# Eighteen small unused loads beside the K and V stream of a decode step

## The chip, the cores and the metric

The kernel runs on one core of a Trainium2 chip. The metric is the device time of one execution in microseconds: median of three runs 195.51 us (195.49 to 195.56). Beside these runs there is one profiled execution, whose span from the first to the last instruction is 194.3 us.

## The reference

A decode step of a parallel block: a layer norm of x (4 batch rows of 512), then attention and a gated feed-forward from the same normalised row, both added to x.

```
W = min(4096, max(256, Sk // 4))            # Sk = 16384, so the last 4096 positions
q = (xn @ wq) in 32 heads of 128            # wq 512 x 4096
k, v = the last W of k_cache, v_cache       # 4 x 8 heads x 4096 x 128, each serves 4 query heads
o = softmax(q k^T / sqrt(128)) v
out = x + o @ wo + (silu(xn @ w_gate) * (xn @ w_up)) @ w_down    # 512 x 1792, 1792 x 512
```

Everything is bfloat16. One execution reads each cached row once: 81 MB, most of them K and V.

## The kernel before

The 32 pairs of batch row and K/V head are taken two at a time, so there are ND = 16 steps. A step loads one K tile and one V tile of 2,048 KB each (128 partitions, 32 positions of 128 numbers for each of two batch rows). K has two buffers (`kbuf`), V two (`vbuf`). In a step TensorE transposes K through an identity (line 397) into PSUM, VectorE copies it to `kT` (line 311), TensorE multiplies with the queries into `ps_s`, takes a row maximum, ScalarE makes the exponential (line 282), and TensorE multiplies with V into `ps_o`. The steps overlap: the product with V of one step runs between the transposes and the scores of the next.

Who issues what, and in which order, is written out by hand. SyncE issues nearly all loads on its own queue: the query weights `wq_sb` (128 partitions of 16,384 numbers, line 253), K 0 and K 1, gate and up weights, V 0, then in a loop `load_k(d)`, `load_v(d - 1)` for d = 2 to 15, the down weights, V 15, and the output weights in five cuts (line 251). `load_k` waits until TensorE has transposed the tile that lay in the buffer (`s_tr`), `load_v` until the product with the old V tile is done (`s_pv`). Both issue at line 177, in a helper. ScalarE issues the load of x and at the end the store of the output, four rows of 1,024 bytes. SyncE waits for that store last (line 512).

GpSimd sets up constants and masks and clears the first V buffer (lines 201 to 233) and has no work after that. `wq_sb` is read by the projection at the start; later its first 1,792 columns are reused for the gate and up products.

Of the kernel before, what the change touches and what calls it, by code (L numbers as in the profile page):

```python
# [12 lines left out]
def bass_parallel_sum__sliding_block_cached__swiglu_ffn__decode_kernel(  # L13
# [10 lines left out]
    out: bass.AP,  # L24
):
    B, _, D = A_x.shape
    _, HKV, Sk, Dh = A_k_cache.shape
    HQ = A_wq.shape[1] // Dh
    F = B_w_gate.shape[1]
# [26 lines left out]
    WQ = sb("wq_sb", [128, NC * HQ * Dh], BF16)  # L56
# [37 lines left out]
    I4 = sb("i4", [B, B], FP32)  # L94
    I4w = sb("i4w", [B, 64], BF16)
    y = sb("y_sb", [B, D], BF16)

    ps = nc.alloc_psum_tensor
    ps_kt = [ps("ps_kt%d" % s, [128, 512], FP32) for s in range(NG)]
# [15 lines left out]
    def sem(name):  # L115
        return nc.alloc_semaphore(name=name)
# [3 lines left out]
    d_wu = sem("d_wu")  # L120
    d_wd = sem("d_wd")
    d_out = sem("d_out")
    WO_CUTS = (0, 16, 22, 29, 31, 32)
    d_wo = [sem("d_wo%d" % q) for q in range(len(WO_CUTS) - 1)]
    d_k = [sem("d_k%d" % s) for s in range(2)]
# [21 lines left out]
    s_pv = sem("s_pv")  # L147
# [14 lines left out]
    wq_ap = A_wq.rearrange("(p c) n -> p (c n)", c=NC)  # L162
# [10 lines left out]
    def load(eng, to, rows, pieces):  # L173


        with nc.discard():
            by_row = eng.dma_start(to, rows).ins  # L177
        whole = replace(by_row.ins[0], ap=pieces.ap, bass_ap=pieces)
        return eng.add_instruction(replace(by_row, name=nc.get_next_instruction_name(), ins=[whole],
                                           ant_dge_precooked=False))  # L180

    def fold_rows(w):
        return w.rearrange("(p c) n -> p (c n)", p=32)

    def load_kv(eng, buf, cache, d):
        return load(eng, buf[:, d % 2 * KVN:(d % 2 + 1) * KVN], kv_ap(cache, d, 1), kv_ap(cache, d, FOLD))

    def out_rows(eng, c0, c1):
        for c in range(c0, c1):
            if c in WO_CUTS:  # L190
                eng.wait_ge(d_wo[WO_CUTS.index(c)], 16)
            for n in range(2):
                last = eng.matmul(ps_acc[64 * n:64 * n + B, 0:256], OP[:, c, :], WO[:, c, 256 * n:256 * n + 256],  # L193
                                  start=False, stop=True, skip_group_check=True)
        return last

    with nc.Block() as block:

        @block.gpsimd
        def _(eng):  # L200
            eng.memset(ident[:], 0.0)
            eng.memset(I4[:], 0.0)
            eng.memset(I8[:], 0.0)
            eng.memset(I4w[:], 0.0)
            eng.memset(rep[:], 0.0)
            eng.memset(ones[:], 1.0)
            eng.memset(mkr[:], -BIG)
            eng.memset(mkc[:], 1.0)
            eng.drain()
            eng.affine_select(I4[:], I4[:], pattern=[[-1, B]], compare_op=ALU.not_equal,  # L210
                              fill=1.0, base=0, channel_multiplier=1)
            eng.affine_select(ident[:], ident[:], pattern=[[-1, 128]], compare_op=ALU.not_equal,
                              fill=1.0, base=0, channel_multiplier=1)
            eng.affine_select(I8[:], I8[:], pattern=[[-1, C]], compare_op=ALU.not_equal,
                              fill=1.0, base=0, channel_multiplier=1)
            eng.affine_select(I4w[:], I4w[:], pattern=[[-1, 64]], compare_op=ALU.not_equal,
                              fill=1.0, base=0, channel_multiplier=1)

            eng.affine_select(rep[:], rep[:], pattern=[[1, REP], [-1, 128]], compare_op=ALU.not_equal,
                              fill=1.0, base=0, channel_multiplier=REP)  # L220

            eng.affine_select(mkr[:], mkr[:].rearrange("j (q b i) -> j q b i", b=2, i=FOLD),
                              pattern=[[0, 64 // FOLD], [-1, 2], [0, FOLD]], compare_op=ALU.not_equal,
                              fill=0.0, base=0, channel_multiplier=1)
            eng.affine_select(mkc[:], mkc[:].rearrange("j (b h) -> j b h", b=2),
                              pattern=[[-1, 2], [0, REP]], compare_op=ALU.is_equal,
                              fill=0.0, base=0, channel_multiplier=1)
            eng.memset(XnT[:].bitcast(FP32), 0.0)
            eng.memset(QZ[:].bitcast(FP32), 0.0)
            eng.drain()  # L230
            eng.engine_nop().then_inc(s_const, 1)
            eng.memset(P[:], 1.0)
            eng.memset(VB[:, HKN:].bitcast(FP32), 0.0)  # L233
            eng.drain()
            eng.engine_nop().then_inc(s_const, 1)
            eng.engine_nop().then_inc(d_v[1], 16)

        @block.sync
        def _(eng):
            def load_k(d):  # L240
                if d >= 2:
                    eng.wait_ge(s_tr, 2 * NG * (d - 1))
                load_kv(eng, KB, A_k_cache, d).then_inc(d_k[d % 2], 16)

            def load_v(d):
                eng.wait_ge(s_pv, d + 1)
                load_kv(eng, VB, A_v_cache, d).then_inc(d_v[d % 2], 16)

            def load_wo(n):
                a, b = WO_CUTS[n], WO_CUTS[n + 1]  # L250
                eng.dma_start(WO[:, a:b, :], wo_ap[:, a:b, :]).then_inc(d_wo[n], 16)  # L251

            eng.dma_start(WQ[:], wq_ap).then_inc(d_wq, 16)

            eng.wait_ge(s_xc, 1)
            load_k(0)
            load_k(1)
            load(eng, WG[:], wg_ap, fold_rows(B_w_gate)).then_inc(d_wg, 16)
            load(eng, WU[:], wu_ap, fold_rows(B_w_up)).then_inc(d_wu, 16)
            load_v(0)  # L260
            for d in range(2, ND):
                load_k(d)
                load_v(d - 1)
            load(eng, WD[:], wd_ap, fold_rows(B_w_down)).then_inc(d_wd, 16)
            load_v(ND - 1)
            for n in range(len(d_wo)):
                load_wo(n)
# [99 lines left out]
        def _(eng):  # L367
# [127 lines left out]
            eng.wait_ge(s_op, 1)  # L495
            out_rows(eng, 0, WO_CUTS[2])

# [6 lines left out]

    out_rows(nc.tensor, WO_CUTS[2], NO).then_inc(s_acc, 1)
    nc.vector.wait_ge(s_acc, 1)
# [2 lines left out]
    nc.scalar.activation(y[:, 256:512], ps_acc[64:64 + B, 0:256], ACT.Identity).then_inc(s_y, 1)  # L509
    nc.scalar.wait_ge(s_y, 2)  # L510
    nc.scalar.dma_start(out_ap, y[:]).then_inc(d_out, 16)
    nc.sync.wait_ge(d_out, 16)


# [26 lines left out]
```

## Time and profile before

| What | Value |
|---|---|
| time, median of 3 runs | 195.51 us |
| span of the profiled execution | 194.3 us |
| around the span, to that median | 1.2 us |
| TensorE matmuls busy | 84% of the span |
| VectorE busy | 59% |
| SyncE's queue q1, share of 16 DMA engines | 97.3% |
| read from memory | 81.01 MB, 417 GB/s over the span |
| mean granted TensorE clock | 0.991 |

The page gives the span of the profiled execution, and no time of its own beside it. Busy shares of a matmul engine include work that is pipelined. The sixteen DMA engines each have a ring for SyncE's queue; their share is the time that packets took, over sixteen times the span. A completion of a load is itself a small packet in these counts. The chain of waits follows the work that ended last back to the start, and a wait on a DMA in it covers the time from its issue to its landing, earlier loads in the same rings included.

### The profile page before, as it was taken

What the parts mean: (1) busy time and instruction counts of PE and PEld (TensorE: products, weight loads), DVE (VectorE), ACT (ScalarE), POOL (GpSimd) and SP (SyncE); (2) the same over time, 40 slices, a digit from 0 to 9 for tenths busy, and PEclk for the clock granted to TensorE, in tenths of its full rate; (3) what the DMA queues carried; (4) which work ended last, traced back from release to release, by engine and by line L of the source; (5) the groups of instructions that cost most, each with busy time, mean ns of one, the idle gap of its engine ahead of it and who ended that gap; (6) DMA issues with size and microseconds to landing.
All of it is one profiled execution on the core that took longest, in us unless ns stands there. A gap on an engine that the chain in (4) does not pass through costs nothing.

```text
span 194.3 us, 7749 instructions
## 1 busy us (share of the span) xinstructions
PE 164.1 (84%) x3460; PEld 142.1 (73%) x3461; DVE 115.4 (59%) x250; ACT 17.0 (9%) x27; POOL 10.5 (5%) x23
## 2 busy tenths in 40 slices
PE   0127999949999989898989898989898989898894
PEld 0112988848989878888878887888887888887662
DVE  1004757617677767676767676767676767675530
ACT  5700010100110101010101010101010101010100
POOL 8930000000000000000000000000000000000000
PEclk9999999988999999999999999999999999999999
DMA  6999997999999999999999999999999999999992
GB/s 217 432 432 432 511 452 332 432 437 432 425 432 425 432 432 432 438 445 432 432 432 432 438 432 438 432 438 432 432 432 432 445 432 432 432 428 428 401 400 94
DMA packets 3589, 81.09 MB, mean 417 GB/s; under 512 B 664, under 2 KB 800, under 8 KB 1184
## 3 DMA queue, kind: packets, MB, share of 16 engines
q1 hardware_dynamic: 3568, 81.01, 97.3%
q8 instruction: 4, 0.07, 0.1%
q10 hardware_dynamic: 16, 0.01, 0.0%
q14 instruction: 1, 0.01, 0.0%
HBM read 81.01 MB, written 0.00 MB: 417 GB/s over the span
## 4 chain that ended last, share of the span: by engine, by line
DMA 61%; PE 34%; issue 1%; DVE 1%; SPq 1%; DVEq 0%
DMA kbuf<-in_A_k_cache_dram 46%; PE ps_kt L397 18%; DMA wo_sb<-in_A_wo_dram 9%; PE ps_s L369 8%; DMA wq_sb<-in_A_wq_dram 6%; PE ps_o L369 5%; PE ps_kt L369 2%; PE ps_acc L369 1%; PE ps_acc L193 1%; DVE kT L311 1%; SPq L251 1%; DVE kT L299 0%; SPq L177 0%; DVE y_sb L507 0%; DVE qz L302 0%
## 5 line engine op out<-in xcount | busy, mean ns | idle before, releaser
L311 DVE COPY kT<-ps_kt 128x1024 bf16<-128x1024 bf16 x128 | 79.9, 683 | 27.4 <-PE ps_kt L397 27.3
L397 PE MATMUL ps_kt<-ident,kbuf 128*128 128x128 bf16 x1024 | 65.7, 225 | 10.4 <-DMA kbuf<-in_A_k_cache_dram 10.4
L397 PEld LDWEIGHTS ps_kt<-ident,kbuf 128*128 128x128 bf16 x1024 | 60.1, 101 | 15.8 <-issue 15.8
L369 PE MATMUL ps_o<-p,vbuf 128*128 128x64 bf16 x1120 | 39.2, 195 | 0.0
L369 PEld LDWEIGHTS ps_o<-p,vbuf 128*128 128x128 bf16 x1120 | 36.0, 99 | 1.2
L369 PEld LDWEIGHTS ps_s<-qz,kT 128*128 128x128 bf16 x1024 | 31.4, 98 | 6.7 <-issue 3.7
L369 PE MATMUL ps_s<-qz,kT 128*128 x1024 | 34.7, 192 | 1.2
L282 ACT ACTIVATE p<-ps_s 128x512 bf16<-128x512 f32 x17 | 10.2, 597 | 161.9 <-PE ps_s L369 161.9
L316 DVE TENSOR_REDUCE rm<-ps_s 128x8 bf16<-128x512 f32 x17 | 11.8, 691 | 19.8 <-PE ps_s L369 19.8
L369 PE MATMUL ps_o<-p,ones 128*128 128x128 bf16 (+1 forms) x69 | 7.0, 222 | 2.3 <-DVE qz L302 1.3
L369 PE MATMUL ps_kt<-wq_sb,xnT 128*32 128x512 bf16 x32 | 3.6, 629 | 5.3 <-DMA wq_sb<-in_A_wq_dram 5.3
L369 PEld LDWEIGHTS ps_o<-p,ones 128*128 128x128 bf16 x69 | 4.5, 98 | 3.5 <-issue 2.2
L369 PE MATMUL ps_s<-mkc,mkr 2*128 2x512 bf16 x17 | 6.9, 404 | 0.0
L374 PE MATMUL ps_acc<-i,xn 4*128 4x4 f32 x4 | 0.6, 254 | 7.4 <-ACT xn L279 7.4
L369 PE MATMUL ps_s<-dg,ones 8*128 8x512 bf16 x17 | 6.5, 385 | 0.0
L327 DVE TENSOR_REDUCE den<-ps_o 128x8 f32<-128x128 f32 x18 | 5.0, 275 | 2.5 <-PE ps_o L369 2.5
L369 PEld LDWEIGHTS ps_kt<-wq_sb,xnT 128*32 128x32 bf16 x32 | 1.2, 138 | 6.8 <-issue 6.8
L299 DVE STREAM_TRANSPOSE kT<-ps_kt 128x512 f32<-128x512 f32 x2 | 1.4, 717 | 8.0 <-PE ps_kt L369 8.0
L374 PEld LDWEIGHTS ps_acc<-i,xn 4*128 4x128 f32 x4 | 0.6, 207 | 7.3 <-issue 7.3
L233 POOL MEMSET vbuf<- 128x6144 f32 x1 | 5.2, 5222 | 0.0
L321 DVE TENSOR_REDUCE m<-ps_acc 8x1 f32<-8x128 f32 x17 | 4.6, 270 | 0.3 <-PE ps_acc L369 0.3
L331 DVE TENSOR_TENSOR oT<-ps_o,den 128x8 f32 (+1 forms) x18 | 3.0, 166 | 2.9 <-issue 2.7
(68 smaller groups left out, 48.6 us busy)
## 6 DMA issues: line engine op xcount, KB each, us to landing
kbuf<-in_A_k_cache_dram SPq DMA_DIRECT2D x16, 2048.0 KB, 12.5
vbuf<-in_A_v_cache_dram SPq DMA_DIRECT2D x16, 2048.0 KB, 11.2
wq_sb<-in_A_wq_dram SPq DMA_DIRECT2D x1, 4096.0 KB, 12.3
wo_sb<-in_A_wo_dram SPq DMA_DIRECT2D x1, 2048.0 KB, 14.9
wg_sb<-in_B_w_gate_dram SPq DMA_DIRECT2D x1, 1792.0 KB, 24.2
wu_sb<-in_B_w_up_dram SPq DMA_DIRECT2D x1, 1792.0 KB, 27.6
wd_sb<-in_B_w_down_dram SPq DMA_DIRECT2D x1, 1792.0 KB, 14.9
wo_sb<-in_A_wo_dram SPq DMA_DIRECT2D x1, 896.0 KB, 17.8
```

Source lines behind the costliest of these rows:

```text
L193: last = eng.matmul(ps_acc[64 * n:64 * n + B, 0:256], OP[:, c, :], WO[:, c, 256 * n:256 * n + 256], start=False, stop=True, skip_group_che ...
L233: eng.memset(VB[:, HKN:].bitcast(FP32), 0.0)
L251: eng.dma_start(WO[:, a:b, :], wo_ap[:, a:b, :]).then_inc(d_wo[n], 16)
L282: eng.activation(P[:, d % 2 * PS:d % 2 * PS + SN], ps_S[d % 2][:], ACT.Exp, scale=SCALE).then_inc(s_p, 1)
L299: eng.transpose(qT[:, 512 * n:512 * n + 512], ps_kt[n][:])
L311: eng.tensor_copy(KT[:, u * HKN + 1024 * g:u * HKN + 1024 * (g + 1)], kt_ps[g].rearrange("p a b -> p (a b)")).then_inc(s_ev, 1)
L316: eng.tensor_reduce(RM[:], ps_S[bank][:].rearrange("p (t c) -> p c t", c=C), AX.X, ALU.max).then_inc(s_rm, 1)
L321: eng.tensor_reduce(m8[:], mt_ps, AX.X, ALU.max)
L327: eng.tensor_reduce(den[:], den_ps.rearrange("p (t c) -> p c t", c=C), AX.X, ALU.add)
L331: eng.tensor_tensor(OT[:, 2 * b:2 * b + 2, ds(r * REP, REP)], O_ps.rearrange("p (j h) -> p j h", j=2), den[:].rearrange("p (j h) -> p j h" ...
L369: return eng.matmul(o, l, r, start=start, stop=stop, skip_group_check=True)
L397: last = eng.transpose(kt_ps[g][:, k, :], KB[:, a:a + 128], ident[:])
```

## The change

SyncE gets fourteen more loads, one after each `load_v(d - 1)` of its loop. They read the first columns of the first n rows of the query weights in memory, and write partitions 0 to n - 1 of a stretch of `wq_sb` that nobody reads any more: n is 1 to 13, and 15 in the last round, and a row has 64 + 16n numbers (160 to 608 bytes). All count on one semaphore, for which SyncE waits at the end of the program, ahead of its wait for the output. GpSimd gets four: 3, 5, 7 and 2 partitions with two pieces each of 96, 104, 112 and 120 bytes, each behind a wait for the products with V of steps 5 to 8; they have a semaphore for which nobody waits. No load of the change is used by the computation, and nothing is removed.

```
@@ names
+    scr = WQ[0:16, 4096:8192]
+    scw = WQ[0:16, 8192:9216]
...
@@ gpsimd, at its end
             eng.engine_nop().then_inc(d_v[1], 16)
+            at = 0
+            for i, n in enumerate((3, 5, 7, 2)):
+                eng.wait_ge(s_pv, 6 + i)
+                w = 48 + 4 * i
+                eng.dma_start(scw[0:n, at:at + 2 * w].rearrange("p (a b) -> p a b", b=w),
+                              wq_ap[0:n, 0:512].rearrange("p (a b) -> p a b", b=256)[:, :, 0:w]).then_inc(d_scw, 16)
+                at += 2 * w
@@ sync
             load_v(0)
+            at = 0
             for d in range(2, ND):
                 load_k(d)
                 load_v(d - 1)
+                n = d - 1 if d < 15 else 15
+                w = 64 + 16 * n
+                eng.dma_start(scr[0:n, at:at + w], wq_ap[0:n, 0:w]).then_inc(d_scr, 16)
+                at += w
             load(eng, WD[:], wd_ap, fold_rows(B_w_down)).then_inc(d_wd, 16)
...
     nc.scalar.dma_start(out_ap, y[:]).then_inc(d_out, 16)
+    nc.sync.wait_ge(d_scr, 16 * 14)
     nc.sync.wait_ge(d_out, 16)
```

On SyncE, the end of its loop (`wd_sb` are the down weights, `wo_sb` the output weights), before:

```order
L177 DMA kbuf<-in_A_k_cache_dram 128x1x8192
L177 DMA vbuf<-in_A_v_cache_dram 128x1x8192
L177 DMA wd_sb<-in_B_w_down_dram 128x7168
L177 DMA vbuf<-in_A_v_cache_dram 128x1x8192
L251 DMA wo_sb<-in_A_wo_dram 128x8192
```

and with the change:

```order
L278 DMA wq_sb<-in_A_wq_dram 13x272
L181 DMA kbuf<-in_A_k_cache_dram 128x1x8192
L181 DMA vbuf<-in_A_v_cache_dram 128x1x8192
L278 DMA wq_sb<-in_A_wq_dram 15x304
L181 DMA wd_sb<-in_B_w_down_dram 128x7168
L181 DMA vbuf<-in_A_v_cache_dram 128x1x8192
L262 DMA wo_sb<-in_A_wo_dram 128x8192
```

A small load now stands between each V load and the next K load, and the last one between V and the down weights. GpSimd's program, which ended with the clearing of the V buffer and two markers, now goes on with its four loads:

```order
L237 MEMSET vbuf 128x6144
L239 ISA
L240 ISA
L245 DMA wq_sb<-in_A_wq_dram 3x2x48
L245 DMA wq_sb<-in_A_wq_dram 5x2x52
L245 DMA wq_sb<-in_A_wq_dram 7x2x56
L245 DMA wq_sb<-in_A_wq_dram 2x2x60
```

No other engine's order changes.

More of the change, by code (lines that the diff above doesn't have):

```diff
@@ L122, in bass_parallel_sum__sliding_block_cached__swiglu_ffn__decode_kernel @@
     d_out = sem("d_out")
+    d_scr = sem("d_scr")
+    d_scw = sem("d_scw")
     WO_CUTS = (0, 16, 22, 29, 31, 32)
```

## The prediction

> **What bounds the kernel now.** I read the page's busy slices first, then the queue table.
>
> ```profile
> span 194.3 us, 7749 instructions
> ...
> POOL 8930000000000000000000000000000000000000
> ...
> DMA  6999997999999999999999999999999999999992
> ...
> q1 hardware_dynamic: 3568, 81.01, 97.3%
> ...
> q10 hardware_dynamic: 16, 0.01, 0.0%
> ```
>
> In nearly every slice the 16 DMA engines are busy 90% or more, and SyncE's queue (q1) alone fills 97.3% of their time. GpSimd does nothing after the third slice. A table of windows makes the middle of the program sharper (its last two columns are the DMA share and GB/s):
>
> ```profile
> 80.00:100.00 20.00, 18.48 (x423) 16.59 (x419) 13.25 (x28) 1.20 (x2) 0.00 (x0) 1.00 1.01 436
> 100.00:120.00 20.00, 17.93 (x401) 16.00 (x398) 13.76 (x29) 1.20 (x2) 0.00 (x0) 1.00 1.00 429
> 120.00:140.00 20.00, 18.34 (x407) 16.48 (x408) 13.42 (x29) 1.20 (x2) 0.00 (x0) 1.00 1.01 437
> 140.00:160.00 20.00, 18.48 (x413) 16.61 (x411) 13.68 (x29) 1.20 (x2) 0.00 (x0) 1.00 0.99 428
> ```
>
> The share is 1.00 within the rounding and the mean of the four is 432.5 GB/s, so each DMA engine moves 432.5 / 16 = 27 GB/s, and a 2,048 KB load of K or V takes 2.097 MB / 432.5 GB/s = 4.85 us. TensorE is busy too, but the chain of waits shows who ends last:
>
> ```profile
> 134.66 1.91 PE ps_kt L397 x32
> 136.56 0.02 issue
> 136.58 12.52 DMA kbuf<-in_A_k_cache_dram
> 149.10 0.12 issue
> ...
> 172.37 0.59 SPq L251
> ...
> 173.47 17.78 DMA wo_sb<-in_A_wo_dram
> 191.25 0.04 issue
> 191.30 1.30 PE ps_acc L193 x20
> 192.60 0.02 issue
> 192.62 0.41 DVE y_sb L507
> ```
>
> Of the 12.52 us that a K load needs from its issue, 4.85 are its own bytes; the other 7.7 are earlier loads still in the rings (and the issue itself, 0.53 us). The rings never run dry, and the end is the landing of the output weights' last columns. So the time is bytes over rate plus the ends, and only what occupies a DMA engine, or lets the rings run empty, can move it.
>
> **SyncE's part of the change.** Fourteen more issues, each behind a V load and ahead of the next K load (the last ahead of the down weights). SyncE's own timeline:
>
> ```profile
> 133.01 0.54 SPq L177 DMA_DIRECT2D vbuf<-in_A_v_cache_dram  x1
> 136.58 0.53 SPq L177 DMA_DIRECT2D kbuf<-in_A_k_cache_dram  x1
> ...
> 162.09 0.54 SPq L177 DMA_DIRECT2D vbuf<-in_A_v_cache_dram  x1
> 162.67 0.60 SPq L177 DMA_DIRECT2D wd_sb<-in_B_w_down_dram  x1
> 171.79 0.54 SPq L177 DMA_DIRECT2D vbuf<-in_A_v_cache_dram  x1
> 172.37 2.48 SPq L251 DMA_DIRECT2D wo_sb<-in_A_wo_dram  x5
> ```
>
> An issue costs SyncE 0.50 us (2.48 / 5) to 0.60 us. No row shows one with few partitions; I take 0.5. Between the end of a V issue (133.55) and the next K issue (136.58) SyncE idles 3.03 us waiting for TensorE's transposes, so the 0.5 us is hidden there. If that cover were gone (an issue of over 3 us), K would be issued late by the rest, and the 7.7 us of work in the rings would still feed the engines. The fifteen-row load delays the down weights by 0.5 us; SyncE then idles from 163.3 to 171.8 anyway. Cost of issuing: 0. The added wait for the fourteen at the program's end stands in front of the wait for the output; their bytes landed some 20 us before: 0.
>
> **What the small loads take from the DMA engines.** The bytes: a row of n partitions has 64 + 16n elements of two bytes, so the fourteen carry 46,976 bytes and GpSimd's four another 3,664. Spread evenly that would be 50.6 KB / 432.5 GB/s = 0.12 us. But they are not spread evenly. The nearest rows to a load of few partitions are those of the output store, four rows of 1,024 bytes on ScalarE's queue:
>
> ```profile
> 193.07 0.27 ACTq L511 DMA_DIRECT2D out_dram<-y_sb  x1
> ```
>
> and the queues in the window from 192.4 to 194.3 us, in 40 slices of 47.5 ns:
>
> ```profile
> DMA  0000000000000000000000000000000000000000
> GB/s 0 0 0 0 0 0 0 0 0 0 0 0 0 0 0 0 0 0 0 0 0 0 0 0 0 0 0 0 0 22 22 22 22 0 0 0 0 0 0 0
> DMA packets 8, 0.00 MB, mean 2 GB/s; under 512 B 4, under 2 KB 8, under 8 KB 8
> ...
> q10 hardware_dynamic: 8, 0.00, 0.7%
> ```
>
> Eight packets: four rows and four under 512 bytes, which I read as one completion per engine taking part. Four rows, four completions: one engine per row. They took 0.7% of 16 x 1.9 us = 0.21 us, so a row with its completion is 53 ns; 1,024 bytes at 27 GB/s are 38 of them, which leaves 15 ns fixed. An n-row load then puts one row and one completion on each of n engines. [...] If the same engines are always the first ones, the first takes part in all fourteen: 5,184 bytes / 27 GB/s = 0.19 us and 14 x 15 ns = 0.21 us, together 0.40 us; an engine takes on average 46,976 / 16 bytes = 0.11 us and 106 / 16 pairs x 15 ns = 0.10 us, together 0.21 us. A bound from above comes from the last microsecond of loads, 191.3 to 192.3:
>
> ```profile
> DMA packets 41, 0.04 MB, mean 40 GB/s; under 512 B 7, under 2 KB 36, under 8 KB 41
> ...
> q1 hardware_dynamic: 41, 0.04, 11.4%
> ```
>
> 11.4% of 16 us over 41 packets is 44 ns for any packet; 28 such packets are 1.25 us on the first engine. From below: if the engines that get the rows have slack at the end, nothing.
>
> **Whether that slack is there** is what decides, and the end of the program shows it:
>
> ```profile
> 189.50:190.00 0.50, 0.50 (x14) 0.40 (x12) 0.00 (x0) 0.00 (x0) 0.00 (x0) 1.00 1.05 406
> 190.00:190.25 0.25, 0.25 (x10) 0.21 (x6) 0.00 (x0) 0.00 (x0) 0.00 (x0) 1.00 0.59 221
> 190.50:190.75 0.25, 0.08 (x2) 0.00 (x0) 0.00 (x0) 0.00 (x0) 0.00 (x0) 1.00 0.36 139
> 190.75:191.00 0.25, 0.00 (x0) 0.00 (x0) 0.00 (x0) 0.00 (x0) 0.00 (x0) 1.00 0.29 107
> 191.00:191.25 0.25, 0.00 (x0) 0.00 (x0) 0.00 (x0) 0.00 (x0) 0.00 (x0) 1.00 0.28 107
> 191.50:192.00 0.50, 0.50 (x14) 0.40 (x10) 0.00 (x0) 0.00 (x0) 0.00 (x0) 1.00 0.12 39
> ```
>
> The engines do not finish together. By 190.75 only 0.29 x 16 = 4.6 of them still work, in the last half microsecond about 0.12 x 16 = 2. Eleven of sixteen have over 1 us to spare, and can take the 0.40 us without anyone noticing; the landing waits for the last two. How much is added to these two depends on which they are, and no view numbers them. With equal chances, the last one takes the mean, 0.21 us, whether the rows go to the first engines or to the engines in turn. I put the term at +0.2 us, with both ends kept: 0 and 1.25.
>
> **GpSimd's part.** Its four loads wait for the same counts as the V loads 5 to 8, so they go out while q1 is full; the engine has no other work left and nobody waits for its semaphore before the program's end. Cost on the engines: 3,664 bytes in 34 pieces, at most 34 x 44 ns over 16 engines = 0.09 us each if completions are of the same kind, and likelier a third of it. [...] I take 0, bounded by 0 and 0.1; nothing is removed, so a gain can only come from the stragglers (rival 3).
>
> **Sum.** The span of 194.3 us and the 1.2 us that lie around it in the 195.51 us median, plus 0 for issues, 0.2 for the rings, 0 for GpSimd: 195.7 us.
>
> **Rivals.** (1) *The last engine carries all the rows at the dear price.* The two stragglers may be among the first engines, and a short row may cost as much as a long one: 195.5 + 0.4 to 1.25, say 196.2 us. For it speaks that completions and rows together are 28 packets on one ring; against it, that 14 engines in 16 are not the last, and that 53 ns for the pair is measured with rows 1.7 to 6.4 times as long. It decides from 0.39 us on the last engine.
>
> (2) *A small load empties its ring.* If the engine that has fetched a short row cannot start the next 2,048 KB load's rows until the short one is through, it pays a set-up each time. The output store shows the size: its issue ends at 193.34, its first packet is in slice 29 (193.78), so 0.44 us of nothing. Fourteen of these on one engine are 6.2 us, beyond all slack: 194.3 + 1.2 + 6.2 - 1.3 to 0 = 200.4 to 201.7 us, on the slower side. Against it: in the windows above every full load ends with completions on all 16 rings and the next one follows, at a share of 1.00, so the rings look ahead. [...]
>
> (3) *The stragglers move.* Which engine is late at the end is set by small accidents, instruction fetches among them:
>
> ```profile
> q8 instruction: 2, 0.03, 0.4%
> ```
>
> (in the window from 30 to 60 us: 0.4% of 480 us over two fetches is 0.96 us each, on one engine). Small loads that arrive in between change which engine is late. If the spread shrinks by half of the 1.3 us, the kernel becomes faster: 194.9 us; if one fetch more falls on a late engine, it is 196.4.
>
> (4) *The rows cost nothing on the engine that ends last*: 195.5 us. It is inside my forecast's own range.
>
> **How the numbers follow.** The forecast with (4): 0.66, own range 195.4 to 195.9. (1): 0.15. (2): 0.05. (3): 0.07 faster, 0.07 slower. A measurement of this kernel tells some 0.2%, 0.39 us, from no change, so 195.12 to 195.90 is "same": the forecast with (4), 0.66. Slower is (1), (2) and the slow half of (3): 0.27. Faster is the other half: 0.07. For 8 in 10 I leave out (2), most of (3)'s fast side and the far end of (1): 195.3 to 196.3 us.
>
> **What would show it.** Right: SyncE's issues of the small loads at about 0.5 us, all within the 3.0 us gap, with K issues still 3.57 us behind V issues; a DMA share of 0.99 to 1.01 in the windows from 80 to 160 us; K's landing at 12.5 us; about 212 packets more on q1, half of them completions; the stretch from 190 us on with the same tail, at most 0.4 us later. Wrong: a share of 0.95 or less in the loop (then rings empty, rival 2), K issues later than 3.6 us behind V (issuing is dear), V or K landings that grow by more than 0.4 us, or an end in which the last engine stands out by more than now (rival 1 or 3).

## The result, and the profile after

Thirteen runs of the changed kernel beside thirteen of the kernel before: median 195.94 us against 195.47 us, ratio 1.0054 with a 95% interval of 1.0028 to 1.0080. It is slower, clear of the noise: the medians differ by 0.47 us (0.24%), the ratio says half a per cent because five late runs weigh in it. The median lies in the range that was forecast (195.7, 195.3 to 196.3), but the forecast was "no measurable change", and the runs are not one group: eight lie at 195.76 to 196.05 us, five at 197.68 to 198.41, the late runs. The kernel before stays within 195.30 to 195.66 here. The granted TensorE clock does not separate the two groups: one run at 195.84 us had 0.982, the one at 198.41 us 0.991. (Ratios here and below leave out runs more than 1.5% above a kernel's fastest, so for a kernel that scatters they say less than its median.)

The profiled execution of the changed kernel is of the first group. Its page:

```profile
span 194.7 us, 7767 instructions
...
q1 hardware_dynamic: 3780, 81.05, 97.4%
...
q0 software_dynamic: 128, 0.00, 0.0%
```

SyncE's queue has 3780 - 3568 = 212 packets more: 106 rows and 106 completions, as the prediction counted. SyncE's timeline:

```profile
132.96 0.53 SPq L181 DMA_DIRECT2D vbuf<-in_A_v_cache_dram  x1
133.54 0.53 SPq L278 DMA_DIRECT2D wq_sb<-in_A_wq_dram  x1
136.53 0.54 SPq L181 DMA_DIRECT2D kbuf<-in_A_k_cache_dram  x1
```

The small load is issued in 0.53 us, and K still goes out 3.57 us behind V. Windows of the loop (DMA share and GB/s at the end):

```profile
100.00:120.00 20.00, 18.01 (x405) 16.05 (x401) 13.63 (x29) 1.19 (x2) 0.57 (x1) 1.00 0.99 425
120.00:140.00 20.00, 18.39 (x408) 16.53 (x409) 13.55 (x29) 1.19 (x2) 0.00 (x0) 1.00 1.02 441
140.00:160.00 20.00, 18.46 (x413) 16.60 (x410) 13.72 (x29) 1.19 (x2) 0.00 (x0) 1.00 0.99 425
...
180.00:190.00 10.00, 8.68 (x172) 6.18 (x170) 4.19 (x13) 0.84 (x2) 0.00 (x0) 1.00 0.94 395
```

The last row of the kernel before:

```profile
180.00:190.00 10.00, 8.99 (x178) 6.45 (x181) 4.19 (x13) 0.85 (x2) 0.00 (x0) 1.00 0.98 410
```

The end of the chain of waits, with the change:

```profile
172.34 0.59 SPq L262
...
173.45 18.12 DMA wo_sb<-in_A_wo_dram
191.57 0.04 issue
191.61 1.27 PE ps_acc L197 x20
```

The loop moves 430 GB/s as before, and the output weights are issued at the same moment as before (173.45 against 173.47 us). They take 18.12 us to land instead of 17.78, 0.34 us more. So in this execution the time is lost in the last 20 us, behind the loads of 12, 13 and 15 partitions. (The row from 180 to 190 us alone would not show it: h2 below has 399 GB/s there and loses 0.2 us.)

### The profile page after: what moved, and what is told of

It reads as the page before. It is cut to its first block, busy times and chain, and to the rows that moved or that the text cites. A ratio compares the mean times of both kernels' runs of the same rounds, so it can differ in the third digit from the quotient of the medians.

```text
span 194.7 us, 7767 instructions
## 1 busy us (share of the span) xinstructions
PE 161.9 (83%) x3460; PEld 140.0 (72%) x3461; DVE 115.1 (59%) x250; ACT 17.0 (9%) x27; POOL 12.9 (7%) x27
## 3 DMA queue, kind: packets, MB, share of 16 engines
q1 hardware_dynamic: 3780, 81.05, 97.4%
## 4 chain that ended last, share of the span: by engine, by line
DMA 61%; PE 33%; issue 3%; DVE 1%; SPq 1%; DVEq 0%
DMA kbuf<-in_A_k_cache_dram 46%; PE ps_kt L413 17%; DMA wo_sb<-in_A_wo_dram 9%; PE ps_s L385 8%; DMA wq_sb<-in_A_wq_dram 6%; PE ps_o L385 5%; PE ps_kt L385 2%; PE ps_acc L385 1%; DVE kT L327 1%; PE ps_acc L197 1%; SPq L262 1%; DVE kT L315 0%; SPq L181 0%; DVE y_sb L523 0%; DVE qz L318 0%
## 5 line engine op out<-in xcount | busy, mean ns | idle before, releaser
L413 PE MATMUL ps_kt<-ident,kbuf 128*128 128x128 bf16 x1024 | 64.2, 222 | 12.6 <-DMA kbuf<-in_A_k_cache_dram 10.6
L413 PEld LDWEIGHTS ps_kt<-ident,kbuf 128*128 128x128 bf16 x1024 | 58.6, 99 | 18.1 <-issue 18.1
L385 PE MATMUL ps_o<-p,vbuf 128*128 128x64 bf16 x1120 | 38.4, 193 | 0.0
L385 PEld LDWEIGHTS ps_o<-p,vbuf 128*128 128x128 bf16 x1120 | 35.2, 98 | 1.1
L245 POOL DMA_DIRECT2D wq_sb<-in_A_wq_dram x4 | 2.4, 598 | 91.0 <-PE ps_o L385 91.0
```

The costliest lines, as they stand in the source:

```text
L245: eng.dma_start(scw[0:n, at:at + 2 * w].rearrange("p (a b) -> p a b", b=w), wq_ap[0:n, 0:512].rearrange("p (a b) -> p a b", b=256)[:, :, 0 ...
L385: return eng.matmul(o, l, r, start=start, stop=stop, skip_group_check=True)
L413: last = eng.transpose(kt_ps[g][:, k, :], KB[:, a:a + 128], ident[:])
```

## The experiments

In all of them the computation is complete; only the unused loads differ, and SyncE's wait at the end counts as many as there are. The runs come from five occasions: e1 to e4; e5 to e9; all f; all g; all h. Those of one occasion ran on one chip, beside the kernel before (medians 195.47 to 195.61 us). The kernel before is not free of late runs either: of its 120 runs, the thirteen above included, five lie at 196.5 us or more, one of them, beside the g runs, at 197.31.

| Run | SyncE's small loads | GpSimd's | runs | median us (lowest, highest) | ratio, 95% interval |
|---|---|---|---|---|---|
| e1 | as in the change | no | 12 | 196.06 (195.42, 198.41) | 1.0042 (1.0011, 1.0074) |
| e2 | none | yes | 12 | 195.47 (195.32, 195.64) | 0.9998 (0.9986, 1.0011) |
| e3 | 14 of 16 partitions | no | 6 | 201.53 (198.15, 204.54) | 1.0199 (1.0134, 1.0265) |
| e4 | 14 of 1 partition | no | 12 | 195.53 (195.25, 195.97) | 1.0000 (0.9985, 1.0015) |
| e5 | 14 of 8 | no | 11 | 195.90 (195.50, 196.29) | 1.0017 (1.0009, 1.0026) |
| e6 | 14 of 12 | no | 9 | 195.67 (195.59, 196.60) | 1.0018 (0.9998, 1.0038) |
| e7 | as e3, source rows 1 KB apart | no | 6 | 205.98 (202.25, 209.66) | 1.0424 (1.0381, 1.0467) |
| e9 | as e3, issued by ScalarE | no | 6 | 206.63 (199.42, 208.75) | none given |
| f1 | as e3, all rows 160 bytes | no | 4 | 195.70 (195.54, 195.74) | 1.0000 (0.9978, 1.0023) |
| f2 | as e3, all rows 544 bytes | no | 4 | 208.18 (203.86, 213.40) | 1.0486 (1.0410, 1.0563) |
| f3 | as e3, all at one place | no | 4 | 198.19 (197.94, 198.92) | 1.0135 (1.0107, 1.0164) |
| f4 | as e3, last seven only | no | 4 | 202.94 (199.03, 203.63) | none given |
| g1 | the change without its last three | yes | 12 | 195.60 (195.45, 196.12) | 0.9992 (0.9975, 1.0008) |
| g2 | the change's last three only | yes | 7 | 197.74 (195.57, 198.61) | 1.0044 (1.0007, 1.0080) |
| g3 | as e3, to every eighth partition | no | 10 | 195.95 (195.88, 196.28) | 1.0010 (0.9997, 1.0024) |
| g4 | the change once more | yes | 10 | 195.95 (195.53, 196.02) | 1.0009 (0.9999, 1.0020) |
| h1 | as g2, to every eighth partition | yes | 11 | 195.63 (195.38, 195.88) | 1.0003 (0.9994, 1.0012) |
| h2 | the change's last one only | yes | 11 | 195.70 (195.54, 195.85) | 1.0011 (1.0002, 1.0020) |

**Which engine's loads.** e1 leaves GpSimd's loop out, e2 SyncE's loads with their wait at the end; e3 and, with 1 for 16, e4 are e1 with

```
-                eng.dma_start(scr[0:n, at:at + w], wq_ap[0:n, 0:w]).then_inc(d_scr, 16)
+                eng.dma_start(scr[0:16, at:at + w], wq_ap[0:16, 0:w]).then_inc(d_scr, 16)
```

> SyncE's fourteen loads alone, without GpSimd's four. The changed kernel ran in two groups: eight of thirteen runs at 195.8 to 196.05 us, five at 197.7 to 198.4; the kernel before stays within 195.3 to 195.7. Theory A (the rows and completions on SyncE's rings make both the 0.4 us and the late group): the same two groups as with the change. Theory B (GpSimd's software queue makes the late group, SyncE's rows only the 0.2 to 0.4 us): all runs at 195.7 to 196.0 us, none above 196.5. Theory C (GpSimd's queue makes all of it): 195.3 to 195.7 us, like before.

> GpSimd's four loads alone, without SyncE's fourteen. Theory A: 195.3 to 195.7 us, like before. Theory B: most runs near 195.5, a good third near 197.5. Theory C: the same as the change, 195.9 us and a late group near 197.8.

> [...] Theory A with even cost: every engine loses 0.2 us for bytes and 0.2 us for the fixed part, so 195.8 to 196.0 us, and no late group if unevenness makes it. If the number of small packets (448 instead of 212) and not their unevenness counts, the late group is here more often than in SyncE's loads alone. Theory C: 195.3 to 195.7 us.

> SyncE's fourteen loads, all of one partition, without GpSimd's: 28 packets in all, at most 0.4 us on one engine if it is always the same, nothing on the others. Theory A with the rings' own time: 195.4 to 195.8 us, no late group. If an issue or a load as such, and not its packets, makes the late group: runs at 197.7 here too. Theory C: 195.3 to 195.7 us.

Theory A holds for e1 (four of twelve runs at 197.27 us or more) and e2: GpSimd's loads cost nothing, SyncE's alone are enough for a late group. Fourteen loads on one partition cost nothing either. But e3 is nowhere near what the rings' own time allows: 6 us instead of 0.4. Windows of e3's profile:

```profile
95.00:102.00 7.00, 6.21 (x140) 5.73 (x137) 4.07 (x8) 0.60 (x1) 0.00 (x0) 1.00 1.00 431
106.00:113.00 7.00, 5.37 (x124) 5.12 (x121) 4.35 (x7) 0.07 (x1) 0.00 (x0) 1.00 1.01 375
118.00:124.00 6.00, 3.82 (x83) 3.61 (x81) 2.40 (x4) 0.00 (x0) 0.00 (x0) 0.85 1.01 388
160.00:167.00 7.00, 6.92 (x160) 6.15 (x156) 3.97 (x9) 0.60 (x1) 0.00 (x0) 1.00 1.02 436
```

Look at the last two columns: in the second row the engines are busy all the time, share 1.01, but move 375 instead of 431 GB/s. The queue counts of the first two windows:

```profile
DMA packets 117, 3.02 MB, mean 431 GB/s; under 512 B 25, under 2 KB 25, under 8 KB 25
...
q1 hardware_dynamic: 117, 3.02, 99.9%
```

```profile
DMA packets 96, 2.62 MB, mean 375 GB/s; under 512 B 16, under 2 KB 16, under 8 KB 16
...
q1 hardware_dynamic: 96, 2.62, 100.8%
```

In the first, 99.9% of 16 x 7 us over 117 - 25 large packets is 1.21 us for a 32 KB row; in the second, 100.8% of the same over 80 is 1.41 us. (The small ones, 9 to 33 ns each by the packets, are under 0.01 us of that.) No small load passes from 106 to 113 us, and yet the rows take 16% longer: a **slow stretch**, which outlasts the load behind which it began. In the window from 160 to 167 us the rate is back.

The trace also keeps the start and duration of every single packet. In e3's trace the median 32 KB row behind the first six small loads takes 1.21 us, behind the seventh to the thirteenth 1.41, 1.36, 1.36, 1.40, 1.44, 1.21 and 1.41 us, and at least 86% of the rows between two small loads lie within 0.01 us of that median, so it is not one straggling engine. In e3 the passage of a small load thus started a slow stretch (the seventh, 1.21 to 1.41 us), changed its rate (the eighth, 1.41 to 1.36 us) or ended it (the twelfth, 1.44 to 1.21 us). The small packets themselves cost about what the prediction charged: a 160-byte row takes 14 ns, a 608-byte row about 33 ns, a completion 9 ns, all of e3's together 0.46 us per engine.

**How many engines, and does it matter where the rows come from or who issues.** e5 and e6 put 8 and 12 in place of 16. e7 reads the rows from pieces 512 numbers apart; e9 takes the loads out of SyncE's loop and issues them from ScalarE behind its exponentials:

```
-eng.dma_start(scr[0:16, at:at + w], wq_ap[0:16, 0:w])
+eng.dma_start(scr[0:16, at:at + w], wq_ap[0:1, 0:8192].rearrange("o (p c) -> (o p) c", p=16)[:, 0:w])
...
                 eng.activation(P[:, d % 2 * PS:d % 2 * PS + SN], ps_S[d % 2][:], ACT.Exp, scale=SCALE).then_inc(s_p, 1)
+                if 1 <= d < ND - 1:
+                    w = 64 + 16 * (d if d < 14 else 15)
+                    eng.dma_start(scr[0:16, at:at + w], wq_ap[0:16, 0:w]).then_inc(d_scr, 16)
+                    at += w
```

> SyncE's fourteen loads, all of eight partitions, without GpSimd's. In the run with sixteen partitions all K and V rows slow down together: from one small load on, each 32 KB row takes 1.36 to 1.43 us on every DMA engine instead of 1.213, the share of busy stays 1.00, and each further small load sets a new duration, once back to 1.213. Theory P (loads that touch many engines at once shift the engines' places against each other, and in some places their reads of memory get in each other's way until the next shift): the effect grows with the engines touched; with eight of sixteen, whose places against the other eight then move by some 30 ns each time, 195.6 to 198 us, some runs late. Theory R (only rows on nearly all engines, eleven or more, start it, as the changed kernel's profile has it in its last two rounds): 195.4 to 195.9 us, none above 196.5.

> As the run before, with twelve partitions in all fourteen loads. Theory P: 196.5 to 201 us, much spread. Theory R: the same, since twelve is past its threshold. A price per packet alone (336 packets at 15 to 53 ns, 21 per engine): 195.8 to 196.0 us, no spread.

> Sixteen partitions as in the run of 201.5 us, but the sixteen source rows lie 1 KB apart in memory instead of 32 KB. Theory M (the short rows, 32 KB apart, all fall on one part of the memory and that starts the slow stretches): 195.8 to 196.2 us, no slow stretch. Theory P (where the rows come from is nothing, the pause that they put into each engine's stream is all): 198 to 204 us again, GB/s of 370 to 400 in some windows.

> Sixteen partitions, rows 32 KB apart, but issued by ScalarE on its own queue behind the exponentials; SyncE's order is that of the kernel before. Theory Q (the place in SyncE's own rings counts: one more row and completion in each shifts how descriptors are fetched): 195.6 to 196.0 us, no slow stretch. Theory P and theory M: 198 to 204 us again, as the engines are the same.

With eight and with twelve partitions the cost is 0.2%, that is about 0.35 us: nearly twice the prediction's term of 0.2 us, and near the 0.40 us that it has for an engine that carries all fourteen rows. (For twelve the interval includes no change; five of its nine runs lie at 195.59 to 195.67 us, four at 196.27 to 196.60.) No run reaches 197 us, so for twelve both theory P and theory R, in the form that I gave them, fall. Sixteen is slow again with near source rows (median 205.98 us) and from ScalarE's queue (206.63 us): neither the distance of the source rows (theory M) nor the place in SyncE's rings (theory Q) is needed for it.

**Size, number or place.** Edits of e3, for f1 (f2 has 272), f3 and f4:

```
-                w = 64 + 16 * n
+                w = 80
...
-                n = d - 1 if d < 15 else 15
+                for n in ((*range(1, 14), 15) if d == 2 else ()):
...
+                if d > 8:
                     eng.dma_start(scr[0:16, at:at + w], wq_ap[0:16, 0:w]).then_inc(d_scr, 16)
```

> Sixteen partitions, fourteen loads, every row 160 bytes instead of 160 to 608. In all three sixteen-partition runs the first five small loads did nothing and the rows of K and V became slow at the sixth, seventh or eighth (320 to 384 bytes, 100 to 113 us). Theory S (size: rows of some 300 bytes and more start it): 195.7 to 195.9 us, no slow stretch. Theory N (number of loads so far) and theory T (place in the K and V stream, from about 100 us on): 198 to 207 us, first slow rows at 100 to 115 us.

> Sixteen partitions, fourteen loads, every row 544 bytes. Theory S: slow from the first or second small load on, 45 to 60 us, so some 10 us more than the graded rows: 208 to 218 us. Theories N and T: as before, first slow rows at 100 to 115 us, 200 to 208 us.

> Sixteen partitions, the fourteen graded loads issued back to back at one place, behind the second V load (about 33 us). Theory S and theory N, if a slow stretch lasts until the next small load sets a new one: the whole loop slow or the whole loop at full rate, decided once: 195.8 us or up to 15% of 140 us more, 216 us, different from run to run. Theory T: nothing before 100 us; if the place alone is not enough without a small load there, 195.8 to 196.1 us throughout.

> Sixteen partitions, only the last seven graded loads (368 bytes and more, from about 104 us on). Theory N (six or seven must have gone before): 195.6 to 195.9 us, no slow stretch or only at the last load. Theories S and T: slow from the first of them on, 199 to 206 us.

Rows of 160 bytes did it in none of four runs (195.54 to 195.74 us). With 544 bytes the slow stretches come and go, as windows of f2 show:

```profile
60.00:74.00 14.00, 13.04 (x299) 11.73 (x296) 9.73 (x20) 0.60 (x1) 0.00 (x0) 1.00 0.98 422
76.00:86.00 10.00, 8.21 (x181) 7.28 (x178) 6.14 (x13) 0.60 (x1) 0.00 (x0) 1.00 1.01 374
88.00:96.00 8.00, 6.43 (x154) 6.01 (x151) 5.44 (x10) 0.00 (x0) 0.00 (x0) 1.00 1.04 447
```

That is earlier than 100 us, so theory T falls, but not at the first load, as theory S had it. In these three windows the median 32 KB row takes 1.21, 1.41 and 1.21 us. In f4 the seven suffice, against theory N's six or seven that must go before. What is left of the three theories is that longer rows do it and the shortest do not, and a weaker theory N: in no profile did the first two loads start a stretch (the first that did was the sixth in e9, the seventh in e3, the eighth in e7, the fourth in f2 and f4). f3 pays most of its 2.7 us at its one place and leaves no slow stretch behind:

```profile
40.00:50.00 10.00, 8.54 (x191) 7.72 (x189) 6.18 (x14) 0.60 (x1) 0.00 (x0) 0.98 0.95 369
...
100.00:120.00 20.00, 18.47 (x424) 16.61 (x422) 13.86 (x30) 1.19 (x2) 0.00 (x0) 1.00 1.00 431
```

Its page shows that this is in part another cost:

```profile
span 196.9 us, 7763 instructions
...
q1 hardware_dynamic: 4016, 81.09, 96.6%
```

By SyncE's timeline the fourteen issues in a row take 7.96 us, from 31.19 us on, and the next K load waits for them. The engines are without packets for 3.4% of 196.9 us, 6.7 us, instead of 2.7% of 194.3 us, 5.2 us: by this estimate about 1.5 of the 2.7 us are engines that ran empty.

**The change's own rounds, and the destination.** g1 and g2 (with `n >= 12`) are edits of the change, g3 is one of e3; g4 is the changed kernel:

```
+                if n < 12:
                     eng.dma_start(scr[0:n, at:at + w], wq_ap[0:n, 0:w]).then_inc(d_scr, 16)
...
-                eng.dma_start(scr[0:16, at:at + w], wq_ap[0:16, 0:w]).then_inc(d_scr, 16)
+                eng.dma_start(WQ[0:128:8, 4096 + at:4096 + at + w], wq_ap[0:16, 0:w]).then_inc(d_scr, 16)
```

> The change without its last three loads of SyncE (12, 13 and 15 partitions); GpSimd's four stay. So far: rows of 160 bytes never start a slow stretch, sixteen partitions do, eight and twelve do not, and the profile of SyncE's loads alone has its slow rows behind the loads of 12 and 13. Theory L (the late group at 197.7 to 198.4 us comes from the last three rounds, the 0.2 us of the others from the rings' own time): 195.5 to 195.8 us, no run above 196.5. Theory G (every round adds its share of the late runs): some runs at 197 to 198 us here too.

> The change with only its last three loads of SyncE (12, 13 and 15 partitions) and GpSimd's four. Theory L: two groups as with the change, one at 195.6 to 195.9 us and a third of the runs at 197 to 198.5. If the first eleven have to have gone before: 195.5 to 195.7 us, no late run.

> Sixteen graded loads as in the run of 201.5 us, but the rows go to partitions 0, 8, 16 to 120 instead of 0 to 15. Theory D (sixteen engines that write to the same few neighbouring partitions at once start the slow stretches): 195.8 to 196.2 us. Theory P (the pause in all sixteen streams is enough, wherever the rows go): 198 to 207 us with windows at 370 to 400 GB/s.

> The changed kernel once more beside the two runs above on the same chip. Theories L and G: a third or so of the runs at 197.5 to 198.5 us, the others at 195.8 to 196.1. If its late runs belonged to the other occasion: all at 195.7 to 196.1 us.

Theory L holds as far as that the last three rounds are enough: with them alone five of seven runs are at 197.04 us or more, against one of thirty of the kernel before. That they are needed is not shown: without them the change costs nothing (g1, 0.9992, no late run), but on this occasion the whole change has no late run either (g4). g2's profiled execution is a late one, at 197.74 us. Its windows, and the same of the kernel before behind them:

```profile
160.00:168.00 8.00, 7.92 (x187) 7.07 (x184) 5.72 (x13) 0.60 (x1) 0.00 (x0) 1.00 1.02 439
176.00:184.00 8.00, 5.37 (x128) 3.77 (x125) 4.88 (x14) 0.85 (x2) 0.00 (x0) 1.00 0.93 360
184.00:190.00 6.00, 5.63 (x118) 4.36 (x118) 1.52 (x5) 0.00 (x0) 0.00 (x0) 1.00 0.96 366
```

```profile
160.00:168.00 8.00, 7.84 (x183) 6.91 (x180) 5.54 (x14) 0.60 (x1) 0.00 (x0) 1.00 1.04 446
176.00:184.00 8.00, 6.50 (x166) 4.89 (x163) 4.66 (x13) 0.85 (x2) 0.00 (x0) 1.00 0.96 412
184.00:190.00 6.00, 5.63 (x102) 4.13 (x101) 1.51 (x5) 0.00 (x0) 0.00 (x0) 1.00 0.96 402
```

Behind the last small load the rate falls to 360 GB/s and stays low to the end; no further small load passes that could end it. By the packets, rows of 32 KB take 1.21 us behind the loads of 12 and 13 partitions and 1.36 us behind that of 15, one of the durations that e3 has in its slow stretches. The output weights need

```profile
173.68 19.70 DMA wo_sb<-in_A_wo_dram
193.38 0.04 issue
```

19.70 us instead of 17.78: these are the 2 us of this late run. (In e1's profiled execution, which is not late, 27 rows take 1.25 to 1.33 us around the load of 13, and behind it 1.21 us again.) Theory D fits g3: the same sixteen loads, to every eighth partition instead of neighbouring ones, give 195.88 to 196.28 us in ten runs, where e3 had 198.15 and more in all six.

```profile
101.00:111.00 10.00, 9.21 (x207) 8.28 (x206) 6.63 (x14) 0.60 (x1) 0.00 (x0) 1.00 1.00 430
134.00:144.00 10.00, 9.21 (x215) 8.28 (x212) 6.73 (x15) 0.60 (x1) 0.00 (x0) 1.00 0.99 427
```

So the destination goes with the time here, a median of 195.95 us against 201.53 us, and no row shows by what. Two limits: sixteen neighbouring partitions were not run beside g3 on its chip (on two other chips all 26 runs of e3, e7, e9, f2 and f4 are at 198.15 us or more), and the runs do not tell whether it is the nearness of the rows or which partition each engine writes that counts. g4 comes out as its second expectation has it: 195.53 to 196.02 us, ratio 1.0009, no late run. So the five late runs of the changed kernel belong to their occasion, and on this one the forecast of no measurable change is right. Yet five of seven runs of g2, which has fewer loads, are late on the same chip; the runs do not show what decides.

**The last three, spread, and the last one alone.** h1 and h2 are edits of g2:

```
-                    eng.dma_start(scr[0:n, at:at + w], wq_ap[0:n, 0:w]).then_inc(d_scr, 16)
+                    eng.dma_start(WQ[0:8 * n:8, 4096 + at:4096 + at + w], wq_ap[0:n, 0:w]).then_inc(d_scr, 16)
...
-                if n >= 12:
+                if n == 15:
```

> The last three loads of SyncE (12, 13 and 15 partitions) and GpSimd's four, with SyncE's rows to every eighth partition instead of neighbouring ones. Beside neighbouring partitions five of seven runs were 197 us or more, and the profile of one of them has K, V and output rows slow from the load of 15 to the end. Theory D (neighbouring destinations start the slow stretch): 195.5 to 196.1 us, no run at 197. Theory P (fifteen engines' pause is enough): a third or more of the runs at 197 to 198.6 us.

> Only SyncE's last small load, 15 neighbouring partitions of 608 bytes, and GpSimd's four. If that single load starts the slow stretch (theory D, one load is enough): some runs at 197 to 198.6 us, the others at 195.4 to 195.8. If the loads of 12 and 13 must go before it: 195.3 to 195.8 us throughout, like the kernel before.

With spread destinations there is no late run (none of eleven), as theory D says. But g2 was not run again on this occasion, and h2, with its one load to neighbouring partitions, has none either (none of eleven, +0.1%, 0.2 us). So h1 proves nothing for theory D, and that the load of 15 needs those of 12 and 13 before it fits h2 but is not shown: the whole change had an occasion without late runs too.

## Why the prediction was wrong, point by point

**What bounds the kernel**: right. DMA did (q1 at 97.4% of the engines' time), and nothing else moved.

**SyncE's issues**: right, 0.44 to 0.59 us inside the 3.0 us gap, K at 3.57 us. **GpSimd**: right at 0 (e2: 0.9998); its four issues took it 0.56 to 0.69 us each. **The rows' own time**: 212 packets as counted, at about the price of bytes plus 15 ns a pair (14 + 9 ns for 160 bytes, 33 + 9 ns for 608). The term of 0.2 us is in the right region: about 0.35 us for e5 and e6, 0.2 us for g3, nothing for e4 and g1. The first group of the changed kernel is 0.43 us above the kernel before, twice the term and near the 0.40 us that the prediction had for the first engine before it took the mean over all. That the rows always go to the same first engines is an assumption: no run shows which engine takes which row, or which one was last.

**The step that failed** is the one that let the 27 GB/s of an engine stand as a constant ("the time is bytes over rate plus the ends") and priced a small load at what its packets take. Small loads of 15 and 16 neighbouring partitions left the large rows behind them 12 to 22% slower (median 1.36 us in g2, up to 1.48 us in e9, instead of 1.21 us for 32 KB), in e3 until the twelfth load passed, in g2 to the end. The sum has no term for that. In g2 it happens behind the last load, with some 20 us to go, and costs 2 us; the late runs of the change, 197.68 to 198.41 us, fit that. On an occasion without such runs (g4) the forecast comes out right: whether it fails depends on something that the prediction did not know of.

**Rival 1** (the last engine carries the rows at the dear price) came out near the median, 196.2 against 195.94 us, by luck as far as the runs show: g1, which keeps eleven of the fourteen loads, costs nothing. **Rival 2** (rings run empty) is not what happens in the profiled executions: shares stay at 0.99 to 1.02 in the loop with the change, while f3, with all its loads at one place, falls to 0.95 there, and fourteen loads on one partition cost nothing (e4), where the rival has 0.44 us for each. (In the kernel before, q1 has 656 completions for 41 loads, 16 for each.) **Rival 3** has one event in the kernel before: next to an instruction fetch of 0.95 us, at 182 us, one 16 KB row takes 1.16 us where the other 127 take 0.61. It does not explain the 2 us of g2; there 32 KB rows behind the load of 15 take 1.36 us throughout, not on a straggler alone.

**The views that I named as proof** were badly chosen. I wrote that a share of 0.95 or less would show the forecast wrong. In e3's slow stretch the share was 1.01 (106 to 113 us): each 32 KB packet took longer (1.41 us instead of 1.21), and all that time counted as busy. GB/s in the same row tells.

What stays open: why a short row to neighbouring partitions slows the rows behind it for microseconds after; why the first two loads started it in no profile; and what decides from run to run and occasion to occasion (late: 5 of 13 for the change, 4 of 12 for e1, 0 of 10 for the change again). That the late runs of the changed kernel itself are such stretches is argued from e1 and g2; none of them was profiled.

## What to carry to other kernels

When a kernel streams at the full rate of its DMA engines, price a small load not by its bytes alone but also by what it may do to the stream. In these runs few partitions (up to twelve), short rows (160 bytes) and spread destinations cost 0.2% at most. A late place leaves less of the stream to slow down (argued from g2, where some 20 us were left and the loss was 2 us; not tested). Read the DMA share together with GB/s: in e3 a share of 1.01 at 375 GB/s stood for rows of 1.41 us instead of 1.21, not for the full rate of 431 GB/s. And look at all runs of a kernel, not at its median, when a few of them are late.

## What was not expected of the hardware

Four loads by GpSimd of 2 to 7 partitions made 128 packets, 32 each (q0 of the changed kernel), while their rows are 17 partitions of two pieces. By the packets these are 17 rows (both pieces in one packet), 47 packets of 8 bytes and 64 completions, sixteen for each load. SyncE's loads of n partitions made exactly 2n here (the change: 212 packets for 106 rows; e4: 3596 packets on q1, 28 more than before; g2: 3648, 80 more). GpSimd's loads landed 6.6 to 7.1 us after their issue, in a stretch where the DMA share was 0.99 to 1.02.

In e3 the DMA stream ran for many microseconds at 13% below its rate or worse (375 instead of 431 GB/s from 106 to 113 us, 371 from 134 to 144 us), with all engines busy (share 1.01 and 1.00), after small loads whose row and completion take 23 to 42 ns, and it returned to the full rate behind another one (436 GB/s from 160 to 167 us). The slow rows do not take just any time: in e3, e7, e9, f2, f4 and g2 the median 32 KB row behind a small load is 1.213 us or one of 1.359, 1.396, 1.411, 1.435, 1.461 and 1.484 us (to within 3 ns), and the same values come back on different chips (1.41 us in e3 and f2, 1.36 us in e3 and g2).
